# A window attention with two gated MLPs: the masked scores stay in PSUM until the exponential has read them

## The chip, the cores and the metric

The kernel runs on one core of a Trainium2 chip. The metric is the device time of one execution in microseconds (us). Times of the kernel before: 965.66 us, the median of 3 runs (965.43 to 966.56).

## The reference

The inputs are q, k and v of 4 batches, 8 heads, 576 positions and 64 channels, and the weights of two gated MLPs (512 to 1536 to 512 channels). What is computed, for all 2304 tokens:

```python
scores = q @ k.T / sqrt(64)
scores = where((rel >= 0) & (rel < 64), scores, -1e9)    # rel = query position - key position
scores = scores - max(scores, axis=-1)
attn = exp(scores); attn = attn / (sum(attn, axis=-1) + 1e-9)
x = attn @ v                                   # heads side by side: 2304 x 512
x = (sigmoid(x @ w_gate) * (x @ w_val)) @ w_out
return ((x @ w_a) * (x @ w_b)) @ w_out2
```

The change lies between the second line and the exponential.

## The kernel before

**The work.** The 2304 token rows are 18 attention tiles of 128 rows, called t = 0 to 17. A tile is two sets of 64 queries, and each set sees 128 keys (its own 64 and the 64 before). The function `attention(t, dst, c0)` is a generator: it gives control back after each step, so that a caller can weave several tiles and the MLPs into one another. For one tile TensorE transposes k and q into PSUM (`kps`, `qps`, L136); ScalarE or VectorE moves them to SBUF (`kt`, `qt`, L112 to L116, where q is also multiplied by minus one eighth, so that the scores are negated); 32 small matmuls write the scores (`sps`, L164). The eight heads fall into two halves, e = 0 for the even heads and e = 1 for the odd, and each half has a PSUM tile of its own: `sps[e]` is 128 partitions by four heads by 128 keys, 2 KB per partition, one whole bank.

For each half follow four VectorE instructions (L177), one per head j: each adds the mask (1e30 outside the window) to the negated scores, writes the sum to the SBUF tile `pr[e]`, and leaves the row minimum in `nmax`. Then follow four ScalarE exponentials (L183), in place in `pr[e]`, with the minimum as bias and scale -1; in 14 of the 18 tiles they also leave the row sums (a second, short record per exponential), and in tiles 2, 4, 6 and 9 VectorE sums instead (L199). VectorE forms the reciprocal (L200, L201), GpSimd multiplies `pr[e]` by it (L203), TensorE transposes the result into PSUM (`tps`, L211), an engine moves it to SBUF (`pt`), and TensorE multiplies with v (`xps`, L221). For tiles 0 to 9 ScalarE and VectorE then write x as a high and a low part (`xh` L228, `xl` L230); for tiles 10 to 17 ScalarE writes it alone (L233).

**PSUM.** It has eight banks, in three pools of tiles one bank large: `ps_acc` (2), `ps_gv` (3) and `ps_at` (3). The scores of tiles 0 and 1 lie in `ps_gv`, those of tiles 2 to 17 in `ps_at`. `ps_at` also holds `tps` and `xps` of all tiles, and `kps` and `qps` from tile 4 on (those of tiles 0 to 3 are in `ps_acc`). A tile gets a bank when the last instruction that touched the one before it there is done. Which of the three banks it gets is settled when the program is built, by a planner with times of its own.

**SBUF.** `pr` has four buffers, so a half's buffer comes back two tiles later.

**The order.** Tiles 0 to 9, the decoding of the first weights (they come as 64-bit words; L335 to L362 turn them into pairs of a high and a low part) and the first turns of the first MLP are woven by the string `RAMP`. `in_order()` then ties each engine's instructions to that order, so in this front part no engine can run something later first. Tiles 10 to 17 are fed between the MLP's turns by `attend`, one step at a time. From then on TensorE works through the two MLPs, three matmuls for each product (high by high, high by low, low by high): L389, L442, L489, L708, L768.

**Lines that the change and the prediction touch:** the allocation of `pr[e]` (L175), the four masked reductions (L177 to L180), the exponentials (L183 to L186), the `ps_at` banks that `sps[e]` holds (L158), and the next users of these banks: L134, L209, L216.

Of the kernel before, what the change touches and what calls it, by code (L numbers as in the profile page):

```python
# [10 lines left out]
F32 = mybir.dt.float32  # L11
# [3 lines left out]
AF = mybir.ActivationFunctionType  # L15
# [6 lines left out]
def tile_window_attention_gated_mlps(ctx, tc, q, k, v, w1g, w1v, w1o, w2a, w2b, w2o, out):  # L22
# [4 lines left out]
    P = 128  # L27
    NP = H // 2
# [27 lines left out]
    kts, vs, work, small = pool("kts", 2), pool("vs", 3), pool("work", 2), pool("small", 2)  # L56
# [19 lines left out]
    for e in range(2):  # L76
        rows = slice(e * WIN, (e + 1) * WIN)
        nc.gpsimd.affine_select(
            out=mask_n[rows], in_=mask_n[rows], pattern=[[1, P]], compare_op=ALU.is_ge,
# [3 lines left out]
            out=mask_n[rows], in_=mask_n[rows], pattern=[[-1, P]], compare_op=ALU.is_ge,  # L83
# [4 lines left out]
    def edge_mask(s):  # L88
        m = qp.tile([P, P], F32, tag="mask_s", name="mask_s")
        nc.vector.tensor_copy(m, mask_n)  # L90
        nc.vector.memset(m[s * WIN:(s + 1) * WIN, 0:WIN], MASKED)
        return m
# [25 lines left out]
    def attention(t, dst, c0):  # L118
# [39 lines left out]
        sps = [sp.tile([P, NP, P], F32, tag=s_tag, name=f"sps{t}_{e}") for e in range(2)]  # L158
# [10 lines left out]
        pr = []  # L169
        for e in range(2):  # L170
            if e == 0:
                stat = small.tile([P, 3, 2, NP], F32, tag="stat", name=f"stat{t}")
                ssum, nmax, den = (stat[:, i] for i in range(3))
                mask = edge_mask(starts[0]) if starts else mask_n
            pr.append(work.tile([P, NP, P], F32, tag="pr", bufs=4, name=f"pr{t}_{e}"))  # L175
            for j in range(NP):
                nc.vector.tensor_tensor_reduce(  # L177
                    out=pr[e][:, j, :], in0=sps[e][:, j, :], in1=mask,
                    scale=1.0, scalar=LARGEST, op0=ALU.add, op1=ALU.min, accum_out=nmax[:, e, j:j + 1],
                )  # L180
            yield
            for j in range(NP):
                nc.scalar.activation(  # L183
                    out=pr[e][:, j, :], in_=pr[e][:, j, :], func=AF.Exp, bias=nmax[:, e, j:j + 1], scale=-1.0,
                    accum_out=None if t in OTHERS["sum"] else ssum[:, e, j:j + 1],
                )  # L186
            yield True
# [9 lines left out]
        for e in range(2):  # L197
            if t in OTHERS["sum"]:
# [5 lines left out]
                out=pr[e], in0=pr[e], in1=den[:, e].unsqueeze(2).to_broadcast([P, NP, P]), op=ALU.mult  # L204
# [52 lines left out]
    def attention_units(blk):  # L257
        if blk in BACK:
            if not back:
                back.update(((i, j), quarter(i, j, "xq").bitcast(F32)) for i in range(2) for j in range(2))  # L260
        elif (0, (blk,)) not in x:
            new_x(0, group_of[blk])
        for i in range(TB):
            if blk in BACK:
                half, c0 = divmod((blk - BACK[0]) * N + i * P, W)
                yield blk, attention(blk * TB + i, [back[g, half] for g in range(2)], c0)
            else:
                yield blk, attention(blk * TB + i, x[0, (blk,)], i * P)
# [631 lines left out]
    for n, (ph, fc) in enumerate(steps):  # L900
# [25 lines left out]
        else:  # L926
            for i in range(2 * NP):
                j, sl = i // NP, slice(i % NP * P, (i % NP + 1) * P)
# [44 lines left out]
```

## Time and profile before

One execution was profiled. It took 965.81 us, 0.15 us more than the median of the runs. Its span, from the first to the last instruction of the trace, is 964.0 us, so 1.8 us lie around it.

| engine | busy us | share of the span | instructions |
|---|---|---|---|
| TensorE, matmul (PE) | 945.2 | 98% | 5594 |
| TensorE, weight load (PEld) | 794.5 | 82% | 5594 |
| VectorE (DVE) | 597.9 | 62% | 1193 |
| ScalarE (ACT) | 454.4 | 47% | 1004 |
| GpSimd (POOL) | 320.1 | 33% | 332 |

The shares are means over stages that differ. A row of the trace says when an instruction starts, how long it takes, which line it is from, what it writes and reads, and in brackets how long its engine sat idle before it and whose end it waited for. Successive instructions of one engine overlap a little, so the distance between two starts is shorter than the length of one.

### The profile page before, as it was taken

To read this page: it belongs to the slowest core of one execution; us is meant where nothing else is said; L and a number is where in the kernel's file an instruction comes from. 1 tells how busy PE (TensorE), PEld (TensorE's weight loads), DVE (VectorE), ACT (ScalarE), POOL (GpSimd) and SP (SyncE) were. 2 spreads that over 40 slices of the span, in tenths; PEclk is the share of its full clock that TensorE was granted. 3 is DMA by queue.
4 is the path that set the end of the run, shared out by engine and by line. 5 is a ranking of instruction groups with operands and counts; after the bars stand their busy time and mean duration, and the time that the engine had idled before them with its cause. 6 is when DMAs were issued, how large, how long until landed. Compare 5 with 4: busy or idle time off the path is not lost.

```text
span 964.0 us, 15333 instructions
## 1 busy us (share of the span) xinstructions
PE 945.2 (98%) x5594; PEld 794.5 (82%) x5594; DVE 597.9 (62%) x1193; ACT 454.4 (47%) x1004; POOL 320.1 (33%) x332
## 2 busy tenths in 40 slices
PE   7899999999999999999999999999999999999998
PEld 5798888788888888888888888888888878888886
DVE  6998688866766784565655554435555683455545
ACT  6996466564545565455442333443333434422321
POOL 4543224431222222222120433444330574444400
PEclk8999999999999999999999999999999999999999
DMA  9999887665565665473541456444333663442212
GB/s 225 218 255 314 240 294 237 231 197 175 185 198 170 226 196 163 127 245 121 178 161 77 132 159 211 132 154 153 138 125 131 209 224 117 150 153 92 106 44 87
DMA packets 122843, 167.46 MB, mean 174 GB/s; under 512 B 61840, under 2 KB 86416, under 8 KB 122768
## 3 DMA queue, kind: packets, MB, share of 16 engines
q1 hardware_dynamic: 122768, 166.49, 54.9%
q8 instruction: 44, 0.72, 0.3%
q14 instruction: 31, 0.25, 0.1%
HBM read 106.95 MB, written 55.05 MB: 168 GB/s over the span
## 4 chain that ended last, share of the span: by engine, by line
PE 73%; DVE 4%; DMA 2%; POOL 1%; issue 1%; ACT 1%; SPq 0%; DVEq 0%; POOLq 0%; ACTq 0%
PE qa L708 13%; PE accq L768 12%; PE gps L389 12%; PE vps L389 12%; PE acc L442 8%; PE qb L708 6%; PE accm L489 3%; PE qc L708 3%; DMA kf<-ex 1%; PE xps L221 1%; PE sps L164 1%; DMA wf<-kf 1%; DVE op L650 1%; PE tps L211 1%; DVE gacc L467 1%
## 5 line engine op out<-in xcount | busy, mean ns | idle before, releaser
L348 POOL TENSOR_TENSOR wi<-wi,low 128x512 int32<-128x512 int32 x72 | 103.6, 1439 | 292.7 <-DVE wi L344 247.8
L389 PE MATMUL gps<-xh,wa 128*128 128x512 f32 (+1 forms) x584 | 169.9, 358 | 0.3 <-DVE hr L411 0.3
L389 PE MATMUL vps<-xh,wb 128*128 128x512 f32 (+1 forms) x584 | 166.8, 352 | 0.0
L693 POOL TENSOR_TENSOR wq<-s,wq 128x256 fp32r<-128x256 f32 x96 | 77.5, 811 | 144.7 <-ACT wq L692 144.6
L389 PEld LDWEIGHTS gps<-xh,wa 128*128 128x128 f32 x584 | 104.9, 189 | 16.6 <-DVE hr L411 0.5
L389 PEld LDWEIGHTS vps<-xh,wb 128*128 128x128 f32 x584 | 105.0, 189 | 15.3 <-issue 0.2
L389 PE MATMUL gps<-xl,wa 128*128 128x512 f32 (+1 forms) x292 | 102.8, 352 | 0.0
L389 PE MATMUL vps<-xl,wb 128*128 128x512 f32 (+1 forms) x292 | 102.5, 351 | 0.0
L489 PE MATMUL accm<-hh,wo 128*128 128x512 f32 (+1 forms) x296 | 85.0, 355 | 1.4 <-DVE gacc L467 1.3
L772 DVE TENSOR_TENSOR res<-accq,res 128x512 f32<-128x512 f32 x80 | 54.4, 688 | 49.1 <-PE accq L768 48.9
L726 ACT ACTIVATE r<-qa 128x512 f32<-128x512 f32 x72 | 42.6, 594 | 83.6 <-PE qa L708 80.3
L354 DVE SCALAR_TENSOR_TENSOR ex<-ex,wi 128x512 f32<-128x512 f32 x72 | 51.1, 710 | 40.9 <-ACT ex L338 19.5
L708 PE MATMUL qa<-op,wq 128*128 128x512 f32 x288 | 75.5, 390 | 0.7 <-POOL op L650 0.7
L442 PE MATMUL acc<-wo,hh 128*128 128x512 f32 x240 | 74.6, 392 | 1.5 <-DVE res L772 1.4
L708 PE MATMUL qb<-op,wq 128*128 128x512 f32 x288 | 73.4, 389 | 0.0
L690 POOL TENSOR_TENSOR s<-wf 128x256 f32<-128x256 f32 x48 | 38.2, 795 | 79.3 <-DMA wf<-kf 77.7
L708 PEld LDWEIGHTS qa<-op,wq 128*128 128x128 f32 x288 | 53.9, 188 | 12.2 <-POOL op L650 1.1
L708 PEld LDWEIGHTS qb<-op,wq 128*128 128x128 f32 x288 | 54.1, 188 | 11.2
L389 PEld LDWEIGHTS vps<-xl,wb 128*128 128x128 f32 x292 | 55.2, 189 | 7.6
L489 PEld LDWEIGHTS accm<-hh,wo 128*128 128x128 f32 x296 | 53.0, 189 | 9.7 <-DVE gacc L467 1.8
L389 PEld LDWEIGHTS gps<-xl,wa 128*128 128x128 f32 x292 | 55.2, 189 | 6.9
L400 DVE SCALAR_TENSOR_TENSOR hl<-hr,hh 128x512 fp32r<-128x512 f32 (+1 forms) x73 | 49.1, 672 | 18.4 <-ACT hh L398 18.2
(128 smaller groups left out, 1923.7 us busy)
## 6 DMA issues: line engine op xcount, KB each, us to landing
wa<-ka SPq DMA_DIRECT2D x27, 512.0 KB, 3.2
wb<-kb SPq DMA_DIRECT2D x27, 512.0 KB, 3.5
wo<-ko SPq DMA_DIRECT2D x27, 512.0 KB, 4.2
st_o<-in_moe_w_out_dram SPq DMA_DIRECT2D x24, 512.0 KB, 4.6
kf<-ex SPq DMA_DIRECT2D x48, 256.0 KB, 4.1
ka<-wa SPq DMA_DIRECT2D x24, 512.0 KB, 3.0
kb<-wb SPq DMA_DIRECT2D x24, 512.0 KB, 3.4
ko<-wo SPq DMA_DIRECT2D x24, 512.0 KB, 3.1
```

The lines of the kernel that those rows point to most:

```text
L348: nc.gpsimd.tensor_tensor(out=wi, in0=wi, in1=low, op=ALU.add)
L354: nc.vector.scalar_tensor_tensor(out=wf, in0=wf, scalar=SMALLEST, in1=wi.bitcast(F32), op0=ALU.is_ge, op1=ALU.mult)
L389: nc.tensor.matmul(ps, lhsT=a[:, c * P:(c + 1) * P], rhs=b[:, c, :], start=(n == 0), stop=(n == 3 * NP - 1))
L400: nc.vector.scalar_tensor_tensor(out=hl, in0=hr, scalar=factor, in1=hh.bitcast(F32), op0=ALU.mult, op1=ALU.subtract)
L442: nc.tensor.matmul(ps, lhsT=a[:, m * P:(m + 1) * P], rhs=b, start=begin and n == 0 and (phase == 1 or m % 2 == 0), stop=end and n == 2 and ...
L489: nc.tensor.matmul(ps[:, m], lhsT=a[:, sl], rhs=b, start=k == 0, stop=k == total - 1)
L690: nc.gpsimd.tensor_tensor(out=s, in0=x, in1=y, op=op)
L693: nc.gpsimd.tensor_tensor(out=t[:, 1], in0=s, in1=t[:, 0].bitcast(F32), op=ALU.subtract)
L708: nc.tensor.matmul(ps, lhsT=a[:, c * P:(c + 1) * P], rhs=b[:, c, :], start=first and n == 0, stop=n == 5, skip_group_check=True,)
L726: nc.scalar.activation(out=r, in_=ps, func=AF.Copy)
L768: nc.tensor.matmul(ps, lhsT=a, rhs=b, start=n == 0, stop=n == len(pairs) - 1)
L772: nc.vector.tensor_tensor(out=dst, in0=ps, in1=dst, op=ALU.add)
```

## The change

The four masked reductions of a half write their sums back to where they read the scores, in PSUM, and no longer to `pr[e]`. The exponentials read them there and write `pr[e]` in SBUF, whose buffer is taken at that point and not before the reductions. Operations, their number and their order stay.

```diff
-            pr.append(work.tile([P, NP, P], F32, tag="pr", bufs=4, name=f"pr{t}_{e}"))
             for j in range(NP):
                 nc.vector.tensor_tensor_reduce(
-                    out=pr[e][:, j, :], in0=sps[e][:, j, :], in1=mask,
+                    out=sps[e][:, j, :], in0=sps[e][:, j, :], in1=mask,
                     scale=1.0, scalar=LARGEST, op0=ALU.add, op1=ALU.min, accum_out=nmax[:, e, j:j + 1],
                 )
             yield
+            pr.append(work.tile([P, NP, P], F32, tag="pr", bufs=4, name=f"pr{t}_{e}"))
             for j in range(NP):
                 nc.scalar.activation(
-                    out=pr[e][:, j, :], in_=pr[e][:, j, :], func=AF.Exp, bias=nmax[:, e, j:j + 1], scale=-1.0,
+                    out=pr[e][:, j, :], in_=sps[e][:, j, :], func=AF.Exp, bias=nmax[:, e, j:j + 1], scale=-1.0,
                     accum_out=None if t in OTHERS["sum"] else ssum[:, e, j:j + 1],
                 )
```

## Rows read from the trace of the kernel before

**Rows 1.** Busy time by stage: busy us (x instructions) per engine, TensorE's granted clock, DMA share.
```profile
0.00:25.00 25.00, 16.91 (x186) 14.43 (x186) 16.18 (x74) 15.61 (x52) 11.28 (x21) 0.86 1.01 224
25.00:50.00 25.00, 22.59 (x329) 19.98 (x330) 23.03 (x90) 22.80 (x69) 13.39 (x14) 0.93 0.89 212
50.00:75.00 25.00, 25.00 (x303) 23.00 (x302) 22.65 (x89) 21.42 (x67) 9.38 (x9) 1.00 0.99 260
```
**Rows 2.** Groups by line and shape: out<-in, count | busy us, mean ns | idle before.
```profile
L183 ACT ACTIVATE pr<-pr,stat 128x128 f32<-128x128 f32 x144 | 53.6, 392 | 9.0 <-DVE stat L177 9.0
L344 DVE SCALAR_TENSOR_TENSOR wi<-st_b,wi 128x512 int32<-128x512 int32 x24 | 16.6, 690 | 0.6
L756 DVE TENSOR_TENSOR r<-qb,r 128x512 f32<-128x512 f32 x24 | 16.6, 690 | 60.9 <-ACT r L726 60.9
L177 DVE CUSTOM_DVE_ANT_0 pr<-sps,mask_n 128x128 f32<-128x128 f32 x112 | 24.9, 284 | 0.6 <-PE sps L164 0.4
L398 ACT ACTIVATE hh<-hr 128x256 fp32r<-128x256 f32 x26 | 10.7, 412 | 9.1 <-DVE hr L415 5.0 <-DVE hr L411 4.1
L409 ACT ACTIVATE hr<-gps 128x256 f32<-128x256 f32 x14 | 5.3, 378 | 1.7 <-PE gps L389 1.7
```
**Rows 3.** Timeline of tile 0's scores, masked reductions (first, fourth) and exponentials (first, fourth).
```profile
6.59 1.10 PE L164 MATMUL sps<-kt,qt 64*64 64x128 f32 x32 [0.69 <-ACT qt L116]
...
7.74 0.29 DVE L177 CUSTOM_DVE_ANT_0 pr<-sps,mask_s 128x128 f32<-128x128 f32 x1 [1.14 <-PE sps L164]
...
8.38 0.29 DVE L177 CUSTOM_DVE_ANT_0 pr<-sps,mask_s 128x128 f32<-128x128 f32 x1
...
8.08 0.40 ACT L183 ACTIVATE pr<-pr,stat 128x128 f32<-128x128 f32 x1 [1.54 <-DVE stat L177]
...
9.25 0.38 ACT L183 ACTIVATE pr<-pr,stat 128x128 f32<-128x128 f32 x1
```
**Rows 4.** Timeline, TensorE before tile 2's and tile 3's scores.
```profile
16.39 1.56 PE L164 MATMUL sps<-kt,qt 64*64 64x128 f32 x32 [0.89 <-ACT qt L116]
...
25.38 1.99 PE L164 MATMUL sps<-kt,qt 64*64 64x128 f32 x32 [2.35 <-POOL wi L348]
```
**Rows 5.** Timeline from 27 to 34 us, TensorE, then ScalarE, then VectorE.
```profile
30.66 0.60 PE L136 MATMUL kps<-ident,k 128*128 128x128 f32 x4
31.84 0.66 PE L136 MATMUL qps<-ident,q 128*128 128x128 f32 x4 [0.58 <-DVE xl L230]
...
30.09 0.39 ACT L183 ACTIVATE pr<-pr,stat 128x128 f32<-128x128 f32 x1
...
32.67 0.39 ACT L183 ACTIVATE pr<-pr,stat 128x128 f32<-128x128 f32 x1
...
29.09 0.28 DVE L177 CUSTOM_DVE_ANT_0 pr<-sps,mask_n 128x128 f32<-128x128 f32 x1
...
31.09 0.69 DVE L230 TENSOR_TENSOR xl<-xps,xh 128x512 fp32r<-128x512 f32 x1
```
**Rows 6.** Timeline, tile 4's second half, then tile 6's first half, with TensorE's next transposes.
```profile
38.14 1.26 ACT L183 ACTIVATE pr<-pr,stat 128x128 f32<-128x128 f32 x4
...
38.38 0.60 PE L211 MATMUL tps<-ident,pr 128*128 128x128 f32 x4
40.03 0.63 PE L211 MATMUL tps<-ident,pr 128*128 128x128 f32 x4 [1.05 <-ACT kt L116]
...
50.66 1.28 ACT L183 ACTIVATE pr<-pr,stat 128x128 f32<-128x128 f32 x4
...
51.32 0.66 PE L211 MATMUL tps<-ident,pr 128*128 128x128 f32 x4
```
**Rows 7.** Timeline, tile 12's first half, and TensorE's next use of that bank.
```profile
212.63 0.39 ACT L183 ACTIVATE pr<-pr,stat 128x128 f32<-128x128 f32 x1
...
230.26 0.60 PE L211 MATMUL tps<-ident,pr 128*128 128x128 f32 x4
```
**Rows 8.** Timeline, the longest wait of TensorE between 50 and 700 us.
```profile
179.68 0.50 PE L489 MATMUL accm<-hh,wo 128*128 128x512 f32 x1 [1.27 <-DVE gacc L467]
```

## The prediction

> **What bounds the kernel now.** I read the busy time by stage first. From 50 us on TensorE is busy all the time at the full granted clock; in the first 25 us it is busy 16.91 us and in the next 22.59 [rows 1], so 10.5 us of idle lie in the front part, where the attention tiles 0 to 9 are woven with the first MLP turns. The matmuls are not changed in number or shape, so the end moves by what TensorE's waits gain or lose. In the front part VectorE and ScalarE are nearly full as well (23.03 and 22.80 of 25 us in the second stretch) [rows 1], and the order of each engine is tied: what comes late there stays late. So I then read the timeline of that part for the waits that the change touches, and last the uses of the `ps_at` banks, one by one, with the end of each one's last reader.
>
> **What it removes.** The exponential's source moves from SBUF to PSUM. No row has an exponential of PSUM, but ScalarE's 128x256 copies stand in both forms: 412 ns from SBUF, 378 ns from PSUM [rows 2], 34 ns less. 144 exponentials by 34 ns are 4.9 us of ScalarE, 80 of them (2.7 us) in the front part. Bounds: nothing, and 50 ns each. I take 34, the nearest rows. ScalarE is off the path after 50 us, so only the front part counts, and there only as part of the chains below.
>
> **What it may add on VectorE.** The masked reductions read PSUM already; their output now goes there too, and no row of this kernel shows VectorE writing PSUM. A half's reductions start 0.64/3 = 0.213 us apart (7.74 to 8.38), and one lasts 0.284 us [rows 2, 3], so 0.07 us of each lies under the next. If the write took that overlap away, a reduction would cost 0.07 us more: 80 in the front part by 0.07 are 5.7 us of VectorE, of which I count half, 2.9 us, on the path. At the other end I allow the 34 ns that ScalarE gains at PSUM, 1.4 us by the same half. VectorE's 128x512 instructions take 690 ns with an operand in PSUM and 690 without [rows 2]. I take 0, the value of these rows.
>
> **A new wait.** A bank seems to be handed from engine to engine whole. Tile 0's first reduction starts at 7.74, right after the last of 32 score matmuls (6.59 + 1.10 = 7.69), though its own four matmuls were the first of them [rows 3]. In SBUF there is no such bond: the first exponential starts at 8.08, while the reductions run until 8.38 + 0.29 = 8.67 [rows 3]. With the sums in PSUM it should start only then, 0.6 us later. Four shorter exponentials give back 0.14, so ScalarE's next instruction is 0.46 late where ScalarE was ahead, and 0.14 early where it was behind. Queued behind it are the moves of the next tile's k and q, for which TensorE waits: before tile 2's scores it idles 0.89 us for ScalarE's `qt` [rows 4]. Tile 0 leaves 0.46 - 0.14 = 0.3 us of lag (its second half was behind), tile 1, which starts in the same way, as much, tile 2 about nothing. Part of it meets idle time of ScalarE. I take 0.5 us at tile 3's scores (25.38 us) [rows 4]; bounds 0 and 0.9 (three times 0.3).
>
> **Banks are held longer.** This is the larger part. A half's bank was free when its fourth reduction had ended; now it is free when its fourth exponential has. For tile 3's second half that is 29.09 + 0.28 = 29.37 before, and 32.67 + 0.39 = 33.06 after [rows 5], 3.7 us more, and `ps_at` has three banks.
> - At 30.66 TensorE transposes tile 4's k, at 31.84 its q [rows 5]. Before, the k took a score bank. After, the three holders are that second half, tile 1's `xps` (VectorE's `xl`, 31.09 + 0.69 = 31.78) and tile 2's `tps`, whose reader comes later. With the lag, less the shorter exponentials, `xl` ends at 32.2 and the exponentials at 33.06 + 0.5 - 0.27 = 33.3. So k starts at 32.2 and q at 33.3, 1.5 us late; TensorE's first MLP turn stands behind it.
> - Tile 4 runs 1.5 us late, its first exponential another 0.6, less 0.2 to 0.3 for eight shorter ones: its second half, which ended at 38.14 + 1.26 = 39.40, ends at about 41.1, and TensorE's transposes of 38.38 [rows 6] find a bank at 40.8 (the next `xl`), 2.4 us late. The next transposes had an idle of 1.05 us before them [rows 6], which goes: 1.3 us are left.
> - Tile 6's first half ended at 50.66 + 1.28 = 51.94, while TensorE's transposes of 51.32 already had its bank [rows 6]. With 1.3 us of lag and a small group wait it ends at 53.4: 2.1 us late, and I add 0.3 (an estimate, from the second half, which is held in the same way) for the transposes after it: 2.4.
>
> From tile 7 on the tiles come farther apart. In tile 12 the first half's exponentials end at 212.63 + 0.39 = 213.02, and TensorE next writes that bank at 230.26 [rows 7]. 17 us of slack cover both the longer hold and the 0.6 us group wait; ScalarE has time to spare there. If that cover were gone, eight tiles by 0.46 would be 3.7 us. The later allocation of `pr` costs nothing: its four buffers come back two tiles later, and the wait for one moves from VectorE to ScalarE.
>
> **The sum.** 0.5, then 1.0 more to reach 1.5, then 0.9 more to reach 2.4 us. TensorE has little idle time later, so the lag stays. Against the profiled execution, 965.81 + 2.4 = 968.2 us; that execution was 0.15 us above the median, so the median should be 968.1 us. The forecast's own range is 967.0 to 969.8: bounds of 0 to 0.9 on the first term, and one bank more or less that the planner happens to choose well.
>
> **Rivals.**
> - *The lag is given back.* At 179.68 TensorE waits 1.27 us for VectorE's `gacc` [rows 8]. If VectorE's decoding is paced by the loads and not by TensorE, a late TensorE finds `gacc` done. Price: 2.4 - 1.27 = 1.1 us left, 966.8; with better bank choices, 965.8. For it: the loads keep their own pace. Against it: VectorE's queue holds MLP work that waits for TensorE in that stretch. Range 965.3 to 967.
> - *VectorE pays for the write.* 2.4 + 2.9 = 5.3 us, 971.0. For it: VectorE is busy 23.03 of 25 us where the tiles are densest [rows 1]. Against it: the equal rows of 690 ns [rows 2].
> - The Trainium skill (Perfetto Trace Analysis, Optimizing Scalar/DVE Operations) speaks for this rival: it gives a fixed overhead of about 125 ns to VectorE at PSUM against 60 at SBUF. No row here shows a VectorE write to PSUM, and the rows with PSUM as source do not show the difference; by that rule 80 reductions would cost 5.2 us of VectorE, an estimate from that page.
> - *Faster: the shorter exponentials win.* ScalarE's queue ends several of TensorE's front waits (0.89 and 1.05 us in [rows 4, 6]). By 40 us some 44 exponentials have saved 44 x 0.034 = 1.5 us of that queue. It decides if no transposes of k or q have to take a score bank that is still being read, that is, if the planner gives tile 4's k and q other banks. Then 965.7 - 1.5 = 964.2. Against it: at 30.66 there are three holders and no other bank.
> - *The change does not bind the exponentials to the whole group.* Then the 0.5 us goes and the banks stay held: 967.6.
>
> **How the numbers follow.** Chances: forecast 0.45, given back 0.25, VectorE pays 0.17, faster 0.10, no group wait 0.03. About 0.2%, 1.9 us, is what a measurement of this kernel can tell from no change: under 963.7 or over 967.6. Slower: 0.7 of the forecast (0.32), all of the third (0.17) and half of the last: 0.50. Faster: the fourth if it gains more than worked out: 0.06. Same: 0.44. The range leaves out the ends of the second rival above 971.0 and of the faster one below 965.0.
>
> **What would show it.** Exponentials shorter by 30 to 40 ns; reductions still 0.213 us apart; the first exponential of tiles 0 and 1 after the fourth reduction; TensorE idle before tile 4's q for ScalarE's exponentials or just behind them, and the first MLP turn about 1.5 us later. The prediction is wrong if tile 4's k and q start where they did, if reductions stand 0.25 us or more apart, or if the first turn after 60 us starts no later than before.

## The result, and the profile after

The changed kernel takes **979.91 us** (median of 4 runs, 978.29 to 981.25) against 965.92 (median of 4, 965.43 to 966.56): ratio 1.0146, 95% interval 1.0134 to 1.0159, so 14.0 us slower. 968.1 was forecast, with a range up to 971.0. The direction was right and the size wrong by a factor of six.

The profiled execution took 981.25 us, 1.3 above the median; its span is 979.5 us. VectorE is busy 610.3 us (597.9 before), ScalarE 450.3 (454.4), TensorE 954.7 (945.2, its front matmuls at a lower clock for longer). Busy time by stage, in the columns of [rows 1]:

```profile
0.00:25.00 25.00, 17.73 (x176) 15.32 (x177) 14.51 (x59) 11.00 (x40) 10.03 (x20) 0.85 0.87 201
25.00:50.00 25.00, 20.86 (x227) 17.39 (x226) 22.22 (x76) 18.65 (x55) 10.39 (x11) 0.67 0.74 176
50.00:75.00 25.00, 21.77 (x296) 19.47 (x293) 21.14 (x81) 18.72 (x57) 9.08 (x9) 1.00 0.90 242
75.00:100.00 25.00, 24.05 (x247) 20.70 (x247) 21.57 (x72) 17.35 (x54) 8.98 (x10) 1.00 0.78 216
```

TensorE now idles until 100 us, where it was full from 50 us on; VectorE and ScalarE are less busy than before in each of the stages of [rows 1]. No engine is at its limit: they wait for one another. The groups, as in [rows 2]:

```profile
L183 ACT ACTIVATE pr<-sps,stat 128x128 f32<-128x128 f32 x144 | 48.7, 374 | 26.6 <-DVE stat L176 23.3 <-PE tps L211 2.6 <-DVE stat L200 0.7
L176 DVE CUSTOM_DVE_ANT_0 sps<-sps,mask_n 128x128 f32<-128x128 f32 x112 | 31.2, 310 | 2.0 <-PE sps L164 0.4
L176 DVE DVE_READ_ACCUMULATOR2_ANT stat<- 128x1 f32 x144 | 20.3, 141 | 0.0
```

An exponential is shorter (392 to 374 ns), but ScalarE waits 23.3 us for the reductions, where it waited 9.0. The third row is the small second record of a masked reduction, which hands the row minimum over; before, it lasted 82 ns:

```profile
L177 DVE DVE_READ_ACCUMULATOR2_ANT stat<- 128x1 f32 x144 | 11.8, 82 | 0.0
```

Tile 0, as in [rows 3] (first VectorE, then ScalarE):

```profile
9.15 0.30 DVE L176 CUSTOM_DVE_ANT_0 sps<-sps,mask_s 128x128 f32<-128x128 f32 x1 [2.31 <-PE sps L164]
9.37 0.14 DVE L176 DVE_READ_ACCUMULATOR2_ANT stat<- 128x1 f32 x1
9.54 0.30 DVE L176 CUSTOM_DVE_ANT_0 sps<-sps,mask_s 128x128 f32<-128x128 f32 x1
...
10.33 0.30 DVE L176 CUSTOM_DVE_ANT_0 sps<-sps,mask_s 128x128 f32<-128x128 f32 x1
10.54 0.14 DVE L176 DVE_READ_ACCUMULATOR2_ANT stat<- 128x1 f32 x1
10.54 0.33 DVE L176 CUSTOM_DVE_ANT_0 sps<-sps,mask_s 128x128 f32<-128x128 f32 x1
...
10.79 0.37 ACT L183 ACTIVATE pr<-sps,stat 128x128 f32<-128x128 f32 x1 [3.72 <-DVE stat L176]
...
11.83 0.37 ACT L183 ACTIVATE pr<-sps,stat 128x128 f32<-128x128 f32 x1
```

The four reductions of a half now start (10.33 - 9.15)/3 = **0.394 us** apart, where it was 0.213. The second starts at 9.54, only when the record before it has ended (9.37 + 0.14 = 9.51). In the kernel before, the second reduction starts together with that record:

```profile
7.96 0.08 DVE L177 DVE_READ_ACCUMULATOR2_ANT stat<- 128x1 f32 x1
7.96 0.29 DVE L177 CUSTOM_DVE_ANT_0 pr<-sps,mask_s 128x128 f32<-128x128 f32 x1
```

The first reduction of the *second* half (10.54) doesn't wait: it works in another bank. The list of the built program (shortened here) shows what the profile doesn't name, since VectorE's wait for itself is a semaphore of its own (DVE_49), which the record that hands the minimum over raises:

```
L176 ISA sps_0_266,stat_284<-sps_0_266,mask_s 128x128 [waits DVE_49,PE_49]
L176 ISA sps_0_266,stat_284<-sps_0_266,mask_s 128x128 [waits DVE_49]
L176 ISA sps_0_266,stat_284<-sps_0_266,mask_s 128x128 [waits DVE_49]
L176 ISA sps_0_266,stat_284<-sps_0_266,mask_s 128x128 [waits DVE_49]
L176 ISA sps_1_267,stat_284<-sps_1_267,mask_s 128x128 [waits PE_49]
```

Before, the second to fourth reduction of a half have no wait. Now each writes a bank that the next one reads, and although the four quarters of the bank don't overlap, the program keeps the order for the whole of it. (Each of these PSUM tiles is exactly one bank, so the runs don't tell whether the bank or the tile is the unit.) A half takes VectorE 10.54 - 9.15 = 1.39 us where it took 0.85. From the first reduction to the end of the fourth exponential it is 12.20 - 9.15 = 3.05 us, where it was 9.63 - 7.74 = 1.89 [rows 3].

The chain of waits of the changed kernel runs straight through this. Pieces of it (start, length, what), and then its shares of the stretch from 5 to 65 us by engine and line:

```profile
9.54 0.30 DVE sps L176
9.84 0.07 DVE stat L176
9.94 0.30 DVE sps L176
...
10.79 1.52 ACT pr L183 x8
12.32 0.18 DVE stat L200
12.53 0.18 DVE stat L201
12.71 0.59 DVE qt L114
13.29 0.14 issue
13.43 1.46 PE sps L164 x32
...
by line: DVE sps L176 18.5%; ACT pr L183 13.0%; PE sps L164 13.0%; PE kps L136 6.5%; PE qps L136 5.6%; PE gps L389 5.4%; DVE stat L176 4.7%; PE tps L211 4.3%; issue 3.9%; DVE xl L230 3.1%; ACT qt L116 2.6%; DVE wi L344 2.3%; DVE pt L114 2.0
```

Tile 1's scores wait for VectorE's `qt`, that for the reciprocal, that for the exponentials, and these for four reductions one by one. The reductions have 18.5 + 4.7 = 23.2% of 60 us, 13.9 us. That is all of their time on the chain, not what the change added; in the kernel before, the chain that ended last has no piece between 5 and 65 us, so there is no share to compare. Setting the starts of the same matmuls in the two timelines side by side shows how late TensorE is (by times of the kernel before): 2.6 us at tile 1's scores, 4.2 at tile 3's, 6.2 at tile 4's k, 11.1 at 52 us, 13.5 at 94 us. Then nothing lasting is added until 171 us (185 us in the changed kernel), where it rises to 18.1 us and falls back to 15.5 by 187 us; it is 15.4 at 574 us. Of this 1.4 us were there before the first changed instruction: in this execution tile 0's scores start 0.53 us later (7.12 against 6.59) and take 1.98 us and not 1.10.

### The profile page after: what moved, and what is told of

Its sections match the earlier page's. It is cut to its first block, busy times and chain, and to the rows that moved or that the text cites. A ratio compares the mean times of both kernels' runs of the same rounds, so it can differ in the third digit from the quotient of the medians.

```text
span 979.5 us, 15345 instructions
## 1 busy us (share of the span) xinstructions
PE 954.7 (97%) x5594; PEld 801.0 (82%) x5594; DVE 610.3 (62%) x1193; ACT 450.3 (46%) x1004; POOL 318.5 (33%) x332
## 4 chain that ended last, share of the span: by engine, by line
PE 85%; DVE 8%; ACT 3%; issue 2%; DMA 1%; POOL 1%; SPq 0%; POOLq 0%; ACTq 0%; DVEq 0%
PE gps L389 15%; PE vps L389 15%; PE qa L708 13%; PE accq L768 12%; PE acc L442 8%; PE accm L489 6%; PE qb L708 6%; PE qc L708 3%; DVE sps L176 2%; PE sps L164 2%; PE xps L221 1%; PE tps L211 1%; ACT pr L183 1%; DMA wf<-kf 1%; PE kps L136 1%
## 5 line engine op out<-in xcount | busy, mean ns | idle before, releaser
L389 PEld LDWEIGHTS vps<-xh,wb 128*128 128x128 f32 x584 | 105.0, 189 | 15.4 <-issue 0.2
```

The costliest lines, as they stand in the source:

```text
L389: nc.tensor.matmul(ps, lhsT=a[:, c * P:(c + 1) * P], rhs=b[:, c, :], start=(n == 0), stop=(n == 3 * NP - 1))
```

## The experiments

All were timed in three rounds beside the kernel before on the same chip. The difference is that of the two medians.

| run | what it has of the change | us | before | difference | 95% of the ratio |
|---|---|---|---|---|---|
| a_wait | reductions wait for one another | 968.18 | 965.97 | +2.2 | 1.0011 to 1.0030 |
| c_group | first exponential waits for all four | 967.43 | 966.26 | +1.2 | 1.0001 to 1.0020 |
| b_hold | exponentials read PSUM (and so wait for all four, and hold the bank) | 969.00 | 965.97 | +3.0 | 1.0024 to 1.0043 |
| ac_wait_group | a_wait and c_group | 971.46 | 966.26 | +5.2 | 1.0037 to 1.0067 |
| ab_wait_hold | a_wait and b_hold | 976.92 | 966.26 | +10.7 | 1.0096 to 1.0126 |
| the change | all, and the write into PSUM | 979.91 | 965.92 | +14.0 | 1.0134 to 1.0159 |
| e_alternate | all, the two halves' reductions in turn | 979.80 | 966.26 | +13.5 | 1.0125 to 1.0155 |
| h_first | the change in tiles 0 to 3 | 971.13 | 966.05 | +5.1 | 1.0042 to 1.0072 |
| c_front | the change in tiles 0 to 9 | 978.45 | 965.97 | +12.5 | 1.0110 to 1.0140 |
| d_back | the change in tiles 10 to 17 | 967.63 | 965.97 | +1.6 | 1.0006 to 1.0025 |
| g_last | the change in tiles 12 to 17 | 965.75 | 966.05 | -0.3 | 0.9992 to 1.0010 |
| f_after_warm | the change, TensorE kept busy | 980.05 | 966.05 | +14.0 | 1.0133 to 1.0163 |
| f_before_warm | none, TensorE kept busy | 965.87 | 966.05 | -0.2 | 0.9990 to 1.0009 |

**The wait of VectorE for itself, alone (a_wait).** The kernel before, with a dependency added between successive reductions of a half:

```diff
+                now = nc.cur_bb.bb.instructions[-1]
+                if j: tc.add_manual_dep(now, prior.name, ...Sync...)
+                prior = now
```

> The kernel before, reductions into SBUF, with one thing added: each masked reduction of a half waits until the one before it on VectorE has ended, as in the changed kernel. If this wait of VectorE for itself is the cause, reductions stand some 0.35 to 0.40 us apart (0.213 before, 0.394 in the changed kernel) and the time goes to 974 to 978 us, at least two thirds of the 14 us. If the longer hold of the score banks is the cause, the reductions slow down alike but the time stays under 968 us.

```profile
8.20 0.29 DVE L177 CUSTOM_DVE_ANT_0 pr<-sps,mask_s 128x128 f32<-128x128 f32 x1 [1.35 <-PE sps L164]
8.54 0.29 DVE L177 CUSTOM_DVE_ANT_0 pr<-sps,mask_s 128x128 f32<-128x128 f32 x1
...
9.20 0.29 DVE L177 CUSTOM_DVE_ANT_0 pr<-sps,mask_s 128x128 f32<-128x128 f32 x1
...
8.54 0.40 ACT L190 ACTIVATE pr<-pr,stat 128x128 f32<-128x128 f32 x1 [1.56 <-DVE stat L177]
```

Tile 0's reductions in that run: 0.333 us apart, so the wait costs 0.12 us of each, and the other 0.06 of the 0.394 are the write into PSUM. Only 2.2 us came of it: the first exponential still starts at 8.54, 0.34 us after the first reduction, and a 0.39 us exponential is slower than a reduction every 0.333. The wait hides behind ScalarE as long as ScalarE need not wait for the fourth.

**The exponentials at PSUM, alone (b_hold).** The reductions write SBUF as before, and the exponentials read the bank of the scores. What lies there is unmasked, so this kernel leaves the mask out of the exponential; ab_wait_hold does too.

```diff
-                    out=pr[e][:, j, :], in_=pr[e][:, j, :], func=AF.Exp, ...
+                    out=pr[e][:, j, :], in_=sps[e][:, j, :], func=AF.Exp, ...
```

> The reductions write to SBUF as before, at their old distance; the exponentials read the unmasked scores in PSUM (the mask is left out of the exponential). So the score banks are held until the last exponential, the exponentials wait for all four reductions and gain PSUM's shorter read, but VectorE neither writes PSUM nor waits for itself. If the held banks and the group wait are the cause: 974 to 980 us. If VectorE's wait for itself is the cause: 965 to 969 us; my forecast of before the run, 968.1, was for this mechanism.

```profile
8.28 0.29 DVE L177 CUSTOM_DVE_ANT_0 pr<-sps,mask_s 128x128 f32<-128x128 f32 x1 [1.43 <-PE sps L164]
...
8.91 0.29 DVE L177 CUSTOM_DVE_ANT_0 pr<-sps,mask_s 128x128 f32<-128x128 f32 x1
...
9.31 0.37 ACT L183 ACTIVATE pr<-sps,stat 128x128 f32<-128x128 f32 x1 [2.24 <-DVE stat L177]
```

The reductions keep their 0.21 us, the exponential starts after the fourth, and the bank is held. These are the two terms that the prediction added up to 2.4 us, and 3.0 were measured.

**Only the wait for four (c_group).** The kernel before, with the first exponential of a half made to wait for the fourth reduction: +1.2 us. The prediction's first term was 0.5, bounds 0 to 0.9; the interval of the measurement is 0.1 to 1.9 us.

> The kernel before, with the first exponential of each half waiting for the half's last reduction and nothing else. By the blind working 0 to 0.9 us: 966 to 967. It splits b_hold's 3.0 us into this wait and the longer hold of the bank (less what the shorter reads give).

**Two and three links together (ac_wait_group, ab_wait_hold).** The edits of the runs above, combined.

> Each reduction (to SBUF) waits for the one before it and the first exponential of a half for its last reduction, but the exponentials read SBUF and the score bank is free after the reductions. Theory 1, the slower half standing whole before ScalarE is the path and the bank does not matter: as ab_wait_hold or 1 us more for the longer SBUF read, 974 to 978 us. Theory 2, the bank held through the exponentials is what turns it into idle time of TensorE: 969 to 971 us.

> Both of the single parts at once: each reduction (to SBUF) waits for the one before it, and the exponentials read the unmasked scores in PSUM (the mask is left out of the exponential), so that they wait for the whole half and hold its bank. Only VectorE's write to PSUM is missing from the changed kernel. Alone they cost 2.2 and 3.0 us. If they add up: 971 us, and the write to PSUM would have to carry 9 us. If they multiply, because the slower half now stands whole before the exponentials and keeps the bank: 975 to 978 us.

2.2 and 1.2 make 5.2, and 2.2 and 3.0 make 10.7: together the links cost far more than their sum. Tile 0 of the last:

```profile
8.27 0.29 DVE L177 CUSTOM_DVE_ANT_0 pr<-sps,mask_s 128x128 f32<-128x128 f32 x1 [1.43 <-PE sps L164]
...
9.28 0.29 DVE L177 CUSTOM_DVE_ANT_0 pr<-sps,mask_s 128x128 f32<-128x128 f32 x1
...
9.68 0.37 ACT L190 ACTIVATE pr<-sps,stat 128x128 f32<-128x128 f32 x1 [2.61 <-DVE stat L177]
```

The wait for the whole half turns three waits of 0.12 us, hidden in a_wait, into 0.36 us ahead of the first exponential, in each half. The step from 10.7 to 14.0 us is what is left for the write itself (0.333 to 0.394 us per reduction, 0.24 us per half).

**Where (c_front, d_back, h_first, g_last).** The change in some tiles only, for instance:

```diff
-                    out=pr[e][:, j, :], in0=sps[e][:, j, :], in1=mask,
+                    out=(sps if t < 10 else pr)[e][:, j, :], in0=sps[e][:, j, :], in1=mask,
```

> The change in tiles 0 to 9 alone. By the staircase of TensorE's lateness in the two traces (13.5 us by 86 us, 2.4 us more at 185 us, 0.4 us given back at 343) this should give 13 to 14 us of loss, 979; were the later tiles the cause, under 970.

> The change in tiles 10 to 17 alone. By the same staircase at most the 2.4 us of tile 11's neighbourhood at 185 us: 965.5 to 968.5. If the loss at 185 us is only the front's lateness meeting other work there, no change: 965.5 to 966.5.

> The change in tiles 0 to 3 alone (8 of the 20 halves of the front part). With the change in tiles 0 to 9 TensorE was 3.4 us late at the scores of tile 3, 6.9 at those of tile 4 and 12.8 at 105 us, and 12.5 us remained at the end. Theory 1 (each halves' wait adds its own part and what is lost stays lost): 971 to 973 us. Theory 2 (a lag from the first tiles is taken up by idle time of the engines later, and the loss is made by tiles 4 to 9): 966 to 969 us.

> The change in tiles 12 to 17 alone. There the planner sets the reductions of the two halves in turn, so that a reduction does not wait for the one just before it (0.25 us from start to start in the changed kernel, 0.39 in tiles 0 to 9). Theory: nothing is lost where the reductions of a half do not follow each other; the 1.6 us of the change in tiles 10 to 17 came from tiles 10 and 11 at 185 us: 965.8 to 966.4 us. Rival: the longer hold of the banks, or the write itself, costs in each tile: 967 us or more.

Tiles 0 to 3 lose 5.1 us, 0.64 per half; tiles 4 to 9 the rest of 12.5, 7.4 us, 0.62 per half. VectorE's longer work is 1.39 - 0.85 = 0.54 us per half. So about as much as VectorE's longer work, and a little more, reaches the end, and nothing is taken up later. In tiles 12 to 17 nothing is lost. There the planner had set the two halves' reductions in turn, as in tiles 10 and 11, and no reduction follows one in its own bank; the rows of the changed kernel at 228 us:

```profile
228.36 0.33 DVE L176 CUSTOM_DVE_ANT_0 sps<-sps,mask_n 128x128 f32<-128x128 f32 x1
...
228.61 0.33 DVE L176 CUSTOM_DVE_ANT_0 sps<-sps,mask_n 128x128 f32<-128x128 f32 x1
```

0.25 us apart: without the wait, the write into PSUM costs 0.037 us. What d_back loses comes at tile 11 (171 us in its trace, 185 in the changed kernel's): TensorE is 0.1 us late before, 4.2 at 174 us, 2.7 behind 180 us and 2.0 from 194 us on. It isn't the self-wait, since the reductions stand in turn here. In the changed kernel TensorE waits there for VectorE's `hl`, which stands between tile 11's reductions, and its granted clock is 0.81 from 185 to 190 us, where the stretch of the kernel before has 1.00:

```profile
187.75 0.50 PE L489 MATMUL accm<-hl,wo 128*128 128x512 f32 x1 [1.33 <-DVE hl L400]
...
185.86 0.33 DVE L176 CUSTOM_DVE_ANT_0 sps<-sps,mask_n 128x128 f32<-128x128 f32 x1
...
186.11 1.59 DVE L400 SCALAR_TENSOR_TENSOR hl<-hr,hh 128x512 fp32r<-128x512 f32 x1
```

**Without the self-wait in the front (e_alternate).** All eight reductions of a tile in the first half's step, the two banks in turn:

```diff
-            for j in range(NP):
+            for j, h in [(j, h) for j in range(NP) for h in range(2) if e == 0]:
```

> The changed kernel with the reductions of the two halves in turn (all eight in the first half's step), so that the reduction before on the same bank has ended when the next one starts: 8 reductions some 0.25 us apart, as in tile 12 of the changed kernel, 2.0 us where they take 2.8. The first half's exponentials stand behind all eight. If VectorE's wait for itself is what makes the loss, at least half of it comes back: 968 to 973 us. If the bank hold and the write to PSUM make it: 977 us or more.

```profile
8.25 0.30 DVE L176 CUSTOM_DVE_ANT_0 sps<-sps,mask_s 128x128 f32<-128x128 f32 x1 [1.40 <-PE sps L164]
8.47 0.33 DVE L176 CUSTOM_DVE_ANT_0 sps<-sps,mask_s 128x128 f32<-128x128 f32 x1
...
9.96 0.33 DVE L176 CUSTOM_DVE_ANT_0 sps<-sps,mask_s 128x128 f32<-128x128 f32 x1
10.21 0.37 ACT L183 ACTIVATE pr<-sps,stat 128x128 f32<-128x128 f32 x1 [3.16 <-DVE stat L176]
```

The expectation was a clear miss. VectorE is through with both halves in 2.0 us and not 2.8, and the kernel is as slow as ever. But the run takes one wait away and puts in another: the first exponential now stands behind seven reductions, since its half's fourth is the seventh in the row: 10.21 - 8.25 = 1.96 us after the first, even later than the 1.64 of the changed kernel. With a_wait (slower reductions, exponentials on time, 2.2 us) this fits a path through how long ScalarE waits for a half, and not through VectorE's time as such; no run shows it by itself.

**The clock (f_after_warm, f_before_warm).** Matmuls of the identity ahead of the scores of tiles 1 to 3, overwritten by them (6, 4 and 10 in f_before_warm):

```diff
+        for _ in range({1: 10, 2: 8, 3: 6}.get(t, 0)):
+            nc.tensor.matmul(sps[0][:, 0, :], lhsT=ident, rhs=ident, start=True, stop=True)
```

> The changed kernel, with matmuls of the identity added on TensorE right ahead of the scores of tiles 1, 2 and 3 (10, 8 and 6 of them, overwritten by the scores), where the trace of the changed kernel has TensorE idle for 2.74, 2.10 and 1.43 us. They do no work that is used. In the changed kernel the granted clock is 0.50 from 22 to 41 us, in the kernel before it is 1.00 from 29 us on. Theory 1: the late clock is a part of the loss, since the first MLP turn runs 1.2 us longer at half clock; with the idle time filled the clock rises earlier and 1 to 3 us come back: 977 to 979 us. Theory 2: in the front part TensorE waits for VectorE and ScalarE in any case, and its clock matters for nothing: 979.5 to 980.5 us, and the clock may rise earlier without effect. If the clock were the main cause: under 974 us.

> The kernel before, with the same kind of added matmuls ahead of the scores of tiles 1, 2 and 3 (6, 4 and 10 of them; its idle times there are 1.48, 1.05 and 2.51 us). Granted clock before: 0.50 to 0.6 from 19 to 28 us. Theory 1 (TensorE's clock counts in the front part): 964 to 965.5 us. Theory 2 (it does not): 965.7 to 966.3 us; if the added matmuls are in the way of the scores, up to 968 us.

Busy time and granted clock (the third number from the end) of the changed kernel and then of f_after_warm:

```profile
25.00:31.00 6.00, 4.03 (x40) 3.28 (x42) 5.79 (x19) 5.18 (x14) 2.20 (x2) 0.50 0.85 189
31.00:37.00 6.00, 4.80 (x53) 3.54 (x46) 5.67 (x24) 4.40 (x17) 2.07 (x3) 0.50 0.76 189
```

```profile
25.00:31.00 6.00, 4.13 (x56) 3.55 (x56) 5.78 (x17) 5.23 (x13) 2.76 (x3) 1.00 0.89 202
31.00:37.00 6.00, 3.09 (x48) 2.58 (x47) 5.75 (x21) 5.40 (x21) 2.48 (x3) 0.99 0.71 194
37.00:43.00 6.00, 6.00 (x85) 5.43 (x85) 4.43 (x16) 2.29 (x5) 2.27 (x2) 0.73 0.90 216
```

From 25 to 37 us the clock was 2.4 and not 1.2 GHz, and not a microsecond came back: TensorE was waiting anyway. The first MLP turn, at 37 us, fell to 1.2 GHz again (in the changed kernel its first 12 matmuls take 2.50 us, and 1.44 in later turns). What that turn's clock is worth can be read from l_after_both below, where the granted clock is 1.00 from 30 to 50 us and the change still costs 12.8 us, so 1.2 of the 14.0 us at most, the moved banks included:

```profile
30.00:40.00 10.00, 7.56 (x123) 6.37 (x122) 9.53 (x31) 8.37 (x27) 3.19 (x5) 1.00 1.03 236
```

Before, too, the clock in the front part is worth nothing that can be measured.

**The banks.** Two pairs moved users out of `ps_at`: the scores of tiles 2 and 3 to `ps_gv` (gv4), the k and q of tiles 4 and 5 to `ps_acc` (acc6), and a third pair did both, each without and with the change. The scores from tile 4 on and all transposes and `xps` stayed in `ps_at`.

```diff
-        kp, kq_tag = (ps_acc, "acc") if t < 4 else (ps_at, "at")
+        kp, kq_tag = (ps_acc, "acc") if t < 6 else (ps_at, "at")
...
-        sp, s_tag = (ps_gv, "gv") if t < 2 else (ps_at, "at")
+        sp, s_tag = (ps_gv, "gv") if t < 4 else (ps_at, "at")
```

> The kernel before, with the scores of tiles 2 and 3 in ps_gv (as those of tiles 0 and 1) and not in ps_at. Order of all engines as before. Both theories: 964 to 967.5 us; less if the banks of ps_at bound the front part already, more if the first MLP turn then waits for ps_gv, which tile 3's scores hold.

> The change, with the scores of tiles 2 and 3 in ps_gv and not in ps_at. Theory 1 (the scores hold ps_at's banks too long, and the transposes of tile 4's k and q wait for them): 3 to 6 us of the 14 come back, 974 to 977 us, and the difference to the kernel before with the same banks is 8 to 11 us. Theory 2 (what is lost is VectorE's and ScalarE's time in a tied order, whatever the banks): the difference stays at 12 to 15 us.

> The kernel before, with the transposed k and q of tiles 4 and 5 in ps_acc (as those of tiles 0 to 3) and not in ps_at. Order of all engines as before. Both theories: 963 to 967 us; more if the first accumulators of the MLP then come late to ps_acc.

> The change, with the transposed k and q of tiles 4 and 5 in ps_acc and not in ps_at. Theory 1 (banks): tile 4's k no longer waits for tile 1's xl (it started 6.2 us late), the difference to the kernel before with the same banks is 9 to 12 us, 974 to 978 us. Theory 2 (time of VectorE and ScalarE): the difference stays at 12 to 15 us, 978 to 981 us.

> The kernel before with both bank moves: the scores of tiles 2 and 3 in ps_gv, the transposed k and q of tiles 4 and 5 in ps_acc. Both theories: 964.5 to 966.5 us (the moves alone gave 965.8 and 965.4).

> The change with both bank moves. Theory 1 (the two shortages stand in for each other): with both gone 3 us or more come back, the difference to the kernel before with both moves is under 10 us, under 976 us. Theory 2 (the chain through the reductions and the exponentials ends last whatever the banks): the difference stays at 12 to 14 us, 977 to 980 us, and between 5 and 65 us the reductions keep over 20% of the chain of waits (23% in the changed kernel).

| moved | without the change | with it | difference |
|---|---|---|---|
| scores of tiles 2, 3 | 965.77 | 978.77 | 13.0 |
| k and q of tiles 4, 5 | 965.36 | 978.43 | 13.1 |
| both | 965.72 | 978.54 | 12.8 |

Tile 4's k starts only 2.2 us late in the last (6.2 in the changed kernel), and yet TensorE is 8.5 us late at 52 us and 10.9 at 94 us. The chain of l_after_both from 5 to 65 us:

```profile
by line: DVE sps L176 21.8%; ACT pr L183 11.7%; DVE wi L344 7.0%; PE sps L164 5.8%; DVE stat L176 5.7%; issue 5.6%; DVE stat L200 4.4%; DVE ex L354 3.9%; DVE stat L199 3.0%; DVE xl L230 3.0%; DVE wi L341 2.9%; PE vps L389 2.4%; PE gps L389 
```

With these users moved, the reductions have 27.5% of the chain and not 23.2, and at most 1.2 us came back, which is no more than the intervals. So the shortage at tiles 2 to 5 that the moves relieve ran beside the chain. The moves don't free the banks that the transposes from tile 4 on need. In l_after_both tile 4's transposes still idle 1.28 us, right behind tile 5's last exponential of a half (51.92 + 0.37 = 52.29):

```profile
51.92 0.37 ACT L183 ACTIVATE pr<-sps,stat 128x128 f32<-128x128 f32 x1
...
52.48 0.63 PE L211 MATMUL tps<-ident,pr 128*128 128x128 f32 x4 [1.28 <-issue]
```

**What stays open.** Why the exponentials' reading of the bank adds 5.5 us to ac_wait_group (5.2 to 10.7), when alone it adds 1.8 to c_group, is not settled. A bank that is free later seems to be a part of it: the changed kernel's transposes start right behind a half's last exponential (55.07 us, behind one that ends at 54.51 + 0.37 = 54.88):

```profile
54.51 0.37 ACT L183 ACTIVATE pr<-sps,stat 128x128 f32<-128x128 f32 x1
...
55.07 0.63 PE L211 MATMUL tps<-ident,pr 128*128 128x128 f32 x4 [1.18 <-issue]
```

In ac_wait_group, which frees the bank after the reductions, the same transposes of tile 4 don't wait:

```profile
50.51 0.60 PE L223 MATMUL tps<-ident,pr 128*128 128x128 f32 x4
```

Idle time ahead of transposes for which the profile names no releaser sums up, in the first 100 us, to 3.6 us in the changed kernel and in l_after_both, 2.4 in ab_wait_hold and none in ac_wait_group. No run gave the transposes other banks, so what it costs is open. Tile 11's loss at 185 us was seen, not taken apart. A version that takes the reductions' self-wait away and keeps the exponentials of a half right behind its own four was not found; none of the runs beats the kernel before by more than 0.2%.

## Why the prediction was wrong

- **"What it may add on VectorE ... I take 0": this is the step that failed.** A reduction costs 0.394 - 0.213 = 0.18 us more, 0.12 for the wait of VectorE for itself (a_wait) and 0.06 for the write. Even the upper bound, 0.07, was less than half: it allowed the overlap to go, and no wait to come. The step looked for the price of the operation in equal rows of 690 ns [rows 2], which read PSUM and don't write it, and not for the order between two of its own instructions. The prediction's own sign of being wrong, reductions 0.25 us or more apart, came true with 0.394.
- **The clue was in the text.** "A bank seems to be handed from engine to engine whole" was used from TensorE to VectorE and from VectorE to ScalarE, but not from VectorE to VectorE.
- **"A new wait" and "Banks are held longer".** For the mechanism as forecast, 2.4 us were worked out, and 3.0 measured (b_hold, inside the forecast's own range of 967.0 to 969.8). How the sum came about is less sure: in the profiled executions b_hold is 1.1 us late at tile 4's q (1.5 forecast, for banks), but c_group, which holds no bank, is 1.9 us late there. And each bound was taken with a half of 0.85 us. With 1.39 us ScalarE waits for the half 1.64 us and not 0.93, and the terms no longer add up. The wait for four was called the smaller part and the banks the larger. With the slower reductions, other banks for the users of tiles 2 to 5, where the prediction had 1.0 of its 2.4 us, bring back 1.2 us at most; the held banks ahead of later transposes, where it had another 0.9, were not taken away by these moves.
- **"TensorE has little idle time later, so the lag stays": right for the lag of the front part.** Between 94 and 171 us it doesn't change for long. The rival that had it given back at `gacc` [rows 8] fell for that lag: c_front is 12.8 us late before that place and 12.8 after, and TensorE waits 1.29 us for `gacc` there as before. What the rival describes does happen to the lag that tile 11 adds just ahead: in the changed kernel and in d_back the wait for `gacc` is gone, and TensorE makes up 1.6 us at that matmul.
- **"From tile 7 on ..." at nothing:** right for tiles 12 to 17 (g_last), wrong for tiles 7 to 9 (11.1 us late at 52 us, 13.5 at 94), and for tile 11. Whether the slack of 17 us or the halves' reductions in turn spare tiles 12 to 17, g_last doesn't tell.
- **The exponentials** came out as forecast: 40 ns from start to start less ((11.83 - 10.79)/3 = 0.347 against (9.25 - 8.08)/3 = 0.390 [rows 3]). It was no help, since ScalarE waited.
- **"The later allocation of `pr` costs nothing": right as far as the runs show.** One exponential waits 2.6 us for a transpose that still reads its buffer (the group row above). But c_front, with the allocation at its old place, has 2.59 us of idle time ahead of the same exponential, put down to the reductions, and c_front and d_back, both with the old place, lose 12.5 + 1.6 = 14.1 us together, as much as the change.
- **The rival "VectorE pays for the write"** came nearest (971.0). Its size was near for the write itself: the hand-over record grew by 141 - 82 = 59 ns. The Trainium skill (Perfetto Trace Analysis, Optimizing Scalar/DVE Operations) gives an overhead of about 60 ns for VectorE at SBUF and 125 at PSUM, 65 more. That is near the 59 ns here, and near the 0.06 us that a reduction costs more where the next one has to wait for its end. Where the next one works in another bank, only 0.037 us are measured.

## What to carry to other kernels

Before an output moves into a buffer that the next instruction of the same engine also touches, ask what unit the order is kept by: here it is a whole PSUM tile of one bank, and four independent quarters became a queue. A wait between instructions that are hidden one by one (2.2 us) comes out much larger as soon as the reader has to wait for the whole group (5.2, where that wait alone costs 1.2), so work out such links together and not as a sum. Where the order of the engines is tied, look at how long a consumer waits for a group, and not only at how busy the producer is.

## What the runs showed of the hardware

- VectorE in PSUM: the record that hands over a reduction's result takes 141 ns and not 82 when the sums go to PSUM; back to back in different banks the reductions are 0.25 us apart and not 0.213.
- A wait of VectorE for its own instruction before costs 0.12 us between reductions that write SBUF (0.213 to 0.333).
- An exponential of 128x128 from PSUM starts the next 40 ns sooner than one from SBUF.
- Tile 0's 32 score matmuls took 1.10 us in most executions and 1.98 in two (the changed kernel's and f_before_warm's), while the trace gave a granted clock of 1.00 in both cases.
